# Twenty-five chunks of 504 or 496 tokens in place of 26 of 480, with every product of two layers issued as two of half the columns

## The chip, the core and the metric

The kernel runs on one core of a Trainium2 chip. The metric is the device time of one execution in microseconds (us). Before the change it is 1017.22 us, the median of three runs (1015.54 to 1017.41).

## The reference, cut to what matters

12480 tokens of 128 channels pass through an attention over 32 inducing points and then through two layers with a hidden width of 2048:

```
h = mab(inducing, x)                        # softmax over all 12480 tokens
x = mab(x, h)                               # softmax over the 32 points, per token
h1 = x @ moe_w_in;    x = max(0.01*h1, h1) @ moe_w_out
h2 = x @ moe2_w_in;   g = h2 if h2 >= 1, 0 if h2 <= -1, else (h2+1)**2/4
y  = g @ moe2_w_out
```

## The kernel before

A head reads all tokens once (nine bands) and forms the 32 rows of `h`. The rest works on chunks of 480 tokens, kept with the channels on the partitions and the tokens as columns. There are 26 chunks, and 16 hidden blocks `j` of 128 in each, so the main loop has 26 x 16 steps `k`, called slots here, and 91 more in which the later stages run out.

One slot issues up to ten large products on TensorE, each of a 128-column weight block (96 rows for the first) with a moving operand of 480 columns:

- stage A (L552): one product, `Gs` with `aT`, which gives a hidden block of the first layer. ScalarE writes its ReLU as `hi` (L555), and VectorE (L562) or, in some slots, GpSimd (L560) writes the rest `lo`.
- stage H (L599): three products (`mm3`, L511 to L513) of the hidden block of four slots earlier. They add into a bank `bX` over the 16 slots of a chunk; a 49th product (L601) ends the chunk.
- stage B (L583): three products that give a hidden block of the second layer, for the chunk that stage A began five chunks (86 slots) earlier. VectorE clamps (L585), ScalarE squares (L566), VectorE adds (L589), ScalarE and GpSimd split the result into `hi` and `lo` (L573, L578).
- stage Y (L611): three products of the block of five slots earlier, added into a bank over 16 slots; then a copy and a store (L614, L615).

`mm3` is three products because each operand is a pair of a high and a low part: high by high, low weight by high, high weight by low. All of them have the type fp32r. The attention of the next chunk is spread over the slots of the current one (`attend`, `scores_g`): small products (L447 or L468, L454, L499), and small operations on VectorE and ScalarE.

The order of instructions on each engine is the order in which the loop writes them. So the main loop has three stretches: one in which only A and H run while weights are still converted (slots 0 to 85), one with all four stages, and one with B and Y alone (the last 91 slots). The helper `warm` (L318) in the head issues products of 256 columns whose result nobody reads; they have the same weights each time.

Of the kernel before, what the change touches and what calls it, by code (L numbers as in the profile page):

```python
# [16 lines left out]
PSUM = bass.MemoryType.PSUM  # L17

N, C, M, FF = 12480, 128, 32, 2048
BT = 120  # L20
NB = N // BT
CB = 4
CW = CB * BT
NCH = NB // CB
SC = 4
NSB = -(-NCH // SC)
NJ = FF // 128
K1 = 3 * M
QW = 512
# [10 lines left out]
LAG = 5  # L40
# [30 lines left out]
def moe_kernel(ctx: ExitStack, tc, x_d, xf_d, xl_d, xt_d, it_d, w1_d, w2_d, w3_d, w4_d, y_d):  # L71


    nc = tc.nc
# [10 lines left out]
    bank = [ps.tile([128, 512], F32, name=f"bank{i}", tag=f"bank{i}") for i in range(8)]  # L85
# [82 lines left out]

    def load_xt(c):
        t = xp.tile([C, CW], F32, name="xt")  # L170
        nc.sync.dma_start(out=t, in_=xt_d[:, c * CW:(c + 1) * CW])
        xts[c] = t


# [264 lines left out]
    def scores_g(c, part):  # L439

        b = bX[c % 2]
        if part == 0:
            t = xts.pop(c)
            if c + 1 < NCH:
                load_xt(c + 1)
            for q in range(CB):
                nc.tensor.matmul(b[q * M:(q + 1) * M, :BT], lhsT=HT[:, 0, :], rhs=t[:, q * BT:(q + 1) * BT],  # L447
                                 start=True, stop=True)
        elif part == 1:
            s = at.tile([128, BT], F32, name="sT")  # L450
            nc.scalar.activation(s, b[:, :BT], AF.Copy)
            st[c] = s
        else:
            nc.tensor.transpose(b[:BT, 128:256], st[c], ident)  # L454

    def attend(c, part):

        b = bX[c % 2]
        if c >= GROUPS:
            if part < 3:  # L460
                return scores_g(c, part)
            part -= 2
        if part == 0:
            t = xts.pop(c)
            if c + 1 < NCH:
                load_xt(c + 1)
            for q in range(CB):
                nc.tensor.matmul(b[:BT, q * M:(q + 1) * M], lhsT=t[:, q * BT:(q + 1) * BT], rhs=HT[:, 0, :],  # L468
                                 start=True, stop=True)
        elif part == 1:  # L470
            at0 = 128 if c >= GROUPS else 0
            sv = b[:BT, at0:at0 + CB * M].rearrange("p (b m) -> p b m", m=M)
            m = at.tile([BT, CB], F32, name="m")
            nc.vector.tensor_reduce(out=m, in_=sv, op=ALU.max, axis=AX.X)
            e = at.tile([BT, CB, M], F32, name="ea")
            nc.vector.tensor_tensor(out=e, in0=sv, in1=m[:, :, None].to_broadcast([BT, CB, M]), op=ALU.subtract)
            st[c] = e
        elif part == 2:
            nc.scalar.activation(st[c], st[c], AF.Exp, scale=SCALE)
        elif part == 3:  # L480
            e = st[c]
            d = at.tile([BT, CB], F32, name="d")
            nc.vector.tensor_reduce(out=d, in_=e, op=ALU.add, axis=AX.X)
            nc.vector.tensor_scalar(out=d, in0=d, scalar1=EPS, scalar2=None, op0=ALU.add)
            nc.vector.reciprocal(out=d, in_=d)
            nc.vector.tensor_tensor(out=e, in0=e, in1=d[:, :, None].to_broadcast([BT, CB, M]), op=ALU.mult)
        elif part == 4:
            e = st[c]
            s = at.tile([BT, CB, 3, M], F32R, name="s")
            nc.scalar.activation(s[:, :, 1, :], e, AF.Copy)  # L490
            if c == 0:
                nc.scalar.activation(s[:, :, 2, :], e, AF.Copy)
            nc.vector.tensor_tensor(out=s[:, :, 0, :], in0=e, in1=s[:, :, 1, :].bitcast(F32), op=ALU.subtract)
            st[c] = s
        elif part == 5:
            s = st.pop(c)
            r = 2 if c else 3
            for q in range(CB):
                nc.tensor.matmul(b[:r * M, q * BT:(q + 1) * BT], lhsT=s[:, q, :r].rearrange("p r m -> p (r m)"),  # L499
                                 rhs=identr[:BT, :BT], start=True, stop=True)  # L500
        elif part == 6:
            t = ap.tile([K1, CW], F32R, name="aT")
            r = 2 if c else 3
            nc.scalar.activation(t[:r * M], b[:r * M, :CW], AF.Copy)
            if c:
                nc.scalar.activation(t[2 * M:], b[M:2 * M, :CW], AF.Copy)
            aT[c] = t

    def mm3(out, n, j, hi, lo, start, stop):
        sl = slice(j * 128, (j + 1) * 128)  # L510
# [22 lines left out]
    for k in range(NS + LAG * NJ + OB + D2):  # L533
# [14 lines left out]
        steps = ATTEND_G if c + 1 >= GROUPS else ATTEND  # L548
        part = steps.index(j) if j in steps and c + 1 < NCH else None
        if in_a:  # L550
            p1 = b1[k % (5 if kb < -2 else 2)][:, :CW]
            nc.tensor.matmul(p1, lhsT=Gs[:, j * 128:(j + 1) * 128], rhs=aT[c], start=True, stop=True)  # L552
            hi = hp1.tile([128, CW], F32R, name="hi1")
            lo = hp1.tile([128, CW], F32R, name="lo1")
            nc.scalar.activation(hi, p1, AF.Relu)  # L555
            h1[k] = hi, lo
            if j in (POOL_LO1 if kb >= 0 else POOL_LO1_FILL if c else POOL_LO1_0):
                r = r1p.tile([128, CW], F32, name="r1")
                nc.scalar.activation(r, p1, AF.Relu)  # L559
                nc.gpsimd.tensor_tensor(out=lo, in0=r, in1=hi.bitcast(F32), op=ALU.subtract)  # L560
            else:
                nc.vector.scalar_tensor_tensor(out=lo, in0=p1, scalar=0.0, in1=hi.bitcast(F32),  # L562
                                               op0=ALU.max, op1=ALU.subtract)
        if kb - 1 in cls:
            sq = ep.tile([128, CW], F32, name="sq")
            nc.scalar.activation(sq, cls.pop(kb - 1), AF.Square, scale=-0.5, bias=half)  # L566
            sqs[kb - 1] = sq
        late = None
        if kb - 2 in gs:
            g = gs.pop(kb - 2)  # L570
            hi = hp3.tile([128, CW], F32R, name="hi3")
            lo = hp3.tile([128, CW], F32R, name="lo3")
            nc.scalar.activation(hi, g, AF.Copy)  # L573
            h3[kb - 2] = hi, lo
            if k >= NS and (kb % DVE_LO3 == 0 or kb > NS - 2):
                late = lo, g, hi
            else:
                nc.gpsimd.tensor_tensor(out=lo, in0=g, in1=hi.bitcast(F32), op=ALU.subtract)  # L578
        if in_b:
            if cb == 0:  # L580
                ensure(2, jb)
            p3 = b3[kb % 3][:, :CW]
            mm3(p3, 1, jb, *x2[cb], True, True)  # L583
            cl = ep.tile([128, CW], F32, name="cl")
            nc.vector.tensor_scalar(out=cl, in0=p3, scalar1=1.0, scalar2=-1.0, op0=ALU.min, op1=ALU.max)  # L585
            cls[kb] = cl
        if kb - 1 in sqs:
            g = ep.tile([128, CW], F32, name="g")
            nc.vector.scalar_tensor_tensor(out=g, in0=b3[(kb - 1) % 3][:, :CW], scalar=-1.0, in1=sqs.pop(kb - 1),  # L589
                                           op0=ALU.max, op1=ALU.add)  # L590
            gs[kb - 1] = g
        if late:
# [2 lines left out]
        if 0 <= kh < NS:  # L595
            if ch == 0:
                ensure(1, jh)
            px = bX[ch % 2][:, :CW]
            mm3(px, 0, jh, *h1.pop(kh), jh == 0, False)  # L599
            if jh == NJ - 1:  # L600
                nc.tensor.matmul(px, lhsT=Qs, rhs=aT.pop(ch), start=False, stop=True)  # L601
                hi = x2p.tile([128, CW], F32R, name="x2hi")
                lo = x2p.tile([128, CW], F32R, name="x2lo")
                nc.scalar.activation(hi, px, AF.Copy)
                nc.vector.tensor_tensor(out=lo, in0=px, in1=hi.bitcast(F32), op=ALU.subtract)
                x2[ch] = hi, lo
        if 0 <= ky < NS:
            if cy == 0:
                ensure(3, jy)
            py = (bank[3 + cy % 2] if cy > NCH - LAG else bY)[:, :CW]  # L610
            mm3(py, 2, jy, *h3.pop(ky), jy == 0, jy == NJ - 1)  # L611
            if jy == NJ - 1:
                y = yp.tile([128, CW], F32, name="y")
                nc.scalar.activation(y, py, AF.Copy)  # L614
                nc.sync.dma_start(out=y_d[:, cy * CW:(cy + 1) * CW], in_=y)  # L615
        if part is not None:
            attend(c + 1, part)
        if k in HIDDEN:
# [59 lines left out]
```

## Time and profile before

| what | value |
|---|---|
| median of three runs | 1017.22 us (1015.54 to 1017.41) |
| profiled execution, first to last instruction | 1015.2 us |
| TensorE with a product under way | 997.9 us, 98% of the span |
| VectorE, ScalarE, GpSimd busy | 835.4, 833.6, 646.4 us |
| granted TensorE clock, mean | 0.997 |

The profiled execution has a span of 1015.2 us; its own whole time is not listed apart, and the three runs lie 0.3 to 2.2 us above that span. Products overlap in the trace: one of 480 columns is recorded as 380 ns long, while the next begins 217 ns after it. So the busy share of TensorE doesn't say how near it is to its limit, and the distance from start to start does.

### The profile page before, as it was taken

What the parts mean: (1) busy time and instruction counts of PE and PEld (TensorE: products, weight loads), DVE (VectorE), ACT (ScalarE), POOL (GpSimd) and SP (SyncE); (2) the same over time, 40 slices, a digit from 0 to 9 for tenths busy, and PEclk for the clock granted to TensorE, in tenths of its full rate; (3) what the DMA queues carried; (4) which work ended last, traced back from release to release, by engine and by line L of the source; (5) the groups of instructions that cost most, each with busy time, mean ns of one, the idle gap of its engine ahead of it and who ended that gap; (6) DMA issues with size and microseconds to landing.
All of it is one profiled execution on the core that took longest, in us unless ns stands there. A gap on an engine that the chain in (4) does not pass through costs nothing.

```text
span 1015.2 us, 15773 instructions
## 1 busy us (share of the span) xinstructions
PE 997.9 (98%) x5032; PEld 837.3 (82%) x5032; DVE 835.4 (82%) x1494; ACT 833.6 (82%) x1615; POOL 646.4 (64%) x533
## 2 busy tenths in 40 slices
PE   8899999999999999999999999999999999999998
PEld 6577777888888888888888888888888888888887
DVE  5769987878878888887887888788788888789997
ACT  5577777888888888888888888888888888889997
POOL 0034556666666666666666666666676667678886
PEclk9999999999999999999999999999999999999999
DMA  9800000000000000000000000000000000000000
GB/s 355 309 13 21 10 21 1 20 1 20 21 1 20 20 20 1 20 21 1 20 21 0 20 20 20 1 20 20 1 20 21 6 6 11 11 11 11 11 10 20
DMA packets 11523, 29.89 MB, mean 29 GB/s; under 512 B 1408, under 2 KB 8064, under 8 KB 10672
## 3 DMA queue, kind: packets, MB, share of 16 engines
q1 hardware_dynamic: 11440, 28.89, 8.0%
q8 instruction: 39, 0.64, 0.3%
q14 instruction: 44, 0.36, 0.1%
HBM read 22.50 MB, written 6.39 MB: 28 GB/s over the span
## 4 chain that ended last, share of the span: by engine, by line
PE 93%; DVE 4%; ACT 2%; POOL 1%; issue 1%; POOLq 0%; ACTq 0%
PE bank L511 26%; PE bank L513 26%; PE bank L512 26%; PE bank L552 9%; DVE lo L562 1%; PE bank L255 1%; PE bank L267 1%; PE bank L300 1%; ACT hi L555 1%; PE bank L447 1%; PE bank L499 1%; PE bank L601 1%; PE bank L468 1%; PE bank L225 0%; PE bank L318 0%
## 5 line engine op out<-in xcount | busy, mean ns | idle before, releaser
L578 POOL TENSOR_TENSOR lo<-g,hi 128x480 fp32r<-128x480 f32 x408 | 499.9, 1228 | 233.0 <-PE bank L512 139.8
L555 ACT ACTIVATE hi<-bank 128x480 fp32r<-128x480 f32 x416 | 235.9, 573 | 121.9 <-PE bank L552 119.5
L513 PE MATMUL bank<-lo,whi 128*128 128x480 f32 x832 | 316.8, 381 | 2.1 <-POOL lo L560 2.1
L511 PE MATMUL bank<-hi,whi 128*128 128x480 f32 x832 | 316.1, 380 | 0.0
L512 PE MATMUL bank<-hi,wlo 128*128 128x480 f32 x832 | 315.9, 380 | 0.0
L566 ACT ACTIVATE sq<-cl,half 128x480 f32<-128x480 f32 x416 | 288.8, 694 | 10.8 <-DVE cl L585 5.7
L585 DVE TENSOR_SCALAR cl<-bank 128x480 f32<-128x480 f32 x416 | 270.1, 649 | 26.5 <-PE bank L513 21.6
L589 DVE SCALAR_TENSOR_TENSOR g<-bank,sq 128x480 f32<-128x480 f32 x416 | 269.8, 649 | 26.5 <-ACT sq L566 25.1
L562 DVE SCALAR_TENSOR_TENSOR lo<-bank,hi 128x480 fp32r<-128x480 f32 x317 | 205.3, 653 | 92.8 <-ACT hi L555 92.7
L573 ACT ACTIVATE hi<-g 128x480 fp32r<-128x480 f32 x416 | 248.5, 597 | 0.7 <-DVE g L589 0.5
L513 PEld LDWEIGHTS bank<-lo,whi 128*128 128x128 f32 x832 | 156.7, 188 | 28.6 <-POOL lo L560 3.7
L512 PEld LDWEIGHTS bank<-hi,wlo 128*128 128x128 f32 x832 | 156.7, 188 | 24.9
L511 PEld LDWEIGHTS bank<-hi,whi 128*128 128x128 f32 x832 | 157.1, 189 | 23.9 <-ACT y L614 0.4
L552 PE MATMUL bank<-aT,Gs 96*128 96x480 f32 x416 | 166.1, 400 | 1.8 <-DVE lo L562 1.1
L560 POOL TENSOR_TENSOR lo<-r,hi 128x480 fp32r<-128x480 f32 x99 | 123.3, 1246 | 62.8 <-ACT r L559 59.5
L511 PE MATMUL bank<-x2hi,whi 128*128 128x480 f32 x416 | 159.1, 383 | 0.6 <-DVE g L589 0.6
L513 PE MATMUL bank<-x2lo,whi 128*128 128x480 f32 x416 | 158.4, 381 | 0.0
L512 PE MATMUL bank<-x2hi,wlo 128*128 128x480 f32 x416 | 157.7, 379 | 0.0
L552 PEld LDWEIGHTS bank<-aT,Gs 96*128 96x128 f32 x416 | 78.5, 189 | 19.5 <-issue 4.3
L511 PEld LDWEIGHTS bank<-x2hi,whi 128*128 128x128 f32 x416 | 79.1, 190 | 12.1 <-DVE g L589 1.8
L512 PEld LDWEIGHTS bank<-x2hi,wlo 128*128 128x128 f32 x416 | 78.9, 190 | 12.1
L513 PEld LDWEIGHTS bank<-x2lo,whi 128*128 128x128 f32 x416 | 78.2, 188 | 12.6
(120 smaller groups left out, 541.6 us busy)
## 6 DMA issues: line engine op xcount, KB each, us to landing
wraw<-in_w SPq DMA_DIRECT2D x16, 512.0 KB, 10.1
xt<-in_xt SPq DMA_DIRECT2D x26, 240.0 KB, 2.6
out_y<-y SPq DMA_DIRECT2D x26, 240.0 KB, 2.0
xb<-in_x SPq DMA_DIRECT2D x5, 1024.0 KB, 14.0
xl<-in_xl SPq DMA_DIRECT2D x1, 1024.0 KB, 15.0
xb<-in_x SPq DMA_DIRECT2D x2, 256.0 KB, 9.1
xb<-in_x SPq DMA_DIRECT2D x1, 512.0 KB, 4.0
xl<-in_xl SPq DMA_DIRECT2D x1, 256.0 KB, 16.0
```

Source lines behind the costliest of these rows:

```text
L511: nc.tensor.matmul(out, lhsT=whi[n][:, sl], rhs=hi, start=start, stop=False)
L512: nc.tensor.matmul(out, lhsT=wlo[n][:, sl], rhs=hi, start=False, stop=False)
L513: nc.tensor.matmul(out, lhsT=whi[n][:, sl], rhs=lo, start=False, stop=stop)
L552: nc.tensor.matmul(p1, lhsT=Gs[:, j * 128:(j + 1) * 128], rhs=aT[c], start=True, stop=True)
L555: nc.scalar.activation(hi, p1, AF.Relu)
L560: nc.gpsimd.tensor_tensor(out=lo, in0=r, in1=hi.bitcast(F32), op=ALU.subtract)
L562: nc.vector.scalar_tensor_tensor(out=lo, in0=p1, scalar=0.0, in1=hi.bitcast(F32), op0=ALU.max, op1=ALU.subtract)
L566: nc.scalar.activation(sq, cls.pop(kb - 1), AF.Square, scale=-0.5, bias=half)
L573: nc.scalar.activation(hi, g, AF.Copy)
L578: nc.gpsimd.tensor_tensor(out=lo, in0=g, in1=hi.bitcast(F32), op=ALU.subtract)
L585: nc.vector.tensor_scalar(out=cl, in0=p3, scalar1=1.0, scalar2=-1.0, op0=ALU.min, op1=ALU.max)
L589: nc.vector.scalar_tensor_tensor(out=g, in0=b3[(kb - 1) % 3][:, :CW], scalar=-1.0, in1=sqs.pop(kb - 1), op0=ALU.max, op1=ALU.add)
```

## The change

The 26 equal chunks become ten of 504 tokens and fifteen of 496, 25 in all. Every tile has the width of the wider chunk, and every instruction is cut to the chunk's own width `w` (`bt`, a quarter of it, in the attention). Each of the large products in the main loop goes through a new function `mm`, which issues it as two, one over each half of the columns, with the same weights. The core of the diff:

```
-BT = 120
-CW = CB * BT
-NCH = NB // CB
+WIDTHS = (504,) * 10 + (496,) * 15
+NCH = len(WIDTHS)
+CW = max(WIDTHS)
+BT = CW // CB
+AT = [sum(WIDTHS[:c]) for c in range(NCH + 1)]
+PARTS = 2
...
+    def mm(out, w, x, start, stop):
+
+        n = x.shape[1]
+        cuts = [n * i // PARTS for i in range(PARTS + 1)]
+        for i, (a, b) in enumerate(zip(cuts, cuts[1:])):
+            nc.tensor.matmul(out[:, a:b], lhsT=w, rhs=x[:, a:b], start=start and i == 0, stop=stop and i == PARTS - 1)
 
     def mm3(out, n, j, hi, lo, start, stop):
         sl = slice(j * 128, (j + 1) * 128)
-        nc.tensor.matmul(out, lhsT=whi[n][:, sl], rhs=hi, start=start, stop=False)
-        nc.tensor.matmul(out, lhsT=wlo[n][:, sl], rhs=hi, start=False, stop=False)
-        nc.tensor.matmul(out, lhsT=whi[n][:, sl], rhs=lo, start=False, stop=stop)
+        mm(out, whi[n][:, sl], hi, start, False)
+        mm(out, wlo[n][:, sl], hi, False, False)
+        mm(out, whi[n][:, sl], lo, False, stop)
...
-            p1 = b1[k % (5 if kb < -2 else 2)][:, :CW]
-            nc.tensor.matmul(p1, lhsT=Gs[:, j * 128:(j + 1) * 128], rhs=aT[c], start=True, stop=True)
-            hi = hp1.tile([128, CW], F32R, name="hi1")
+            w = WIDTHS[c]
+            p1 = b1[k % (5 if kb < -2 else 2)][:, :w]
+            mm(p1, Gs[:, j * 128:(j + 1) * 128], aT[c], True, True)
+            hi = hp1.tile([128, CW], F32R, name="hi1")[:, :w]
...
-                nc.tensor.matmul(px, lhsT=Qs, rhs=aT.pop(ch), start=False, stop=True)
+                mm(px, Qs, aT.pop(ch), False, True)
```

All other lines of the diff put a chunk's own width in the place of the common one: in the loads of `xt`, the attention, the banks' slices, the tiles of the stages and the store of `y`.

## Rows read from the trace of the kernel before

**Rows 1.** The page: busy time by engine, and the span in 40 slices.

```profile
PE 997.9 (98%) x5032; PEld 837.3 (82%) x5032; DVE 835.4 (82%) x1494; ACT 833.6 (82%) x1615; POOL 646.4 (64%) x533
...
PEclk9999999999999999999999999999999999999999
```

**Rows 2.** The page: shares of the chain that ended last.

```profile
PE 93%; DVE 4%; ACT 2%; POOL 1%; issue 1%; POOLq 0%; ACTq 0%
```

**Rows 3.** Busy us (and instructions) of each engine in three stretches, then granted clock.

```profile
75.00:140.00 65.00, 61.62 (x298) 50.03 (x297) 60.08 (x110) 50.49 (x107) 32.66 (x24) 1.00 0.06 16
250.00:850.00 600.00, 600.00 (x2895) 509.09 (x2894) 492.02 (x867) 505.56 (x982) 404.43 (x333) 1.00 0.05 14
895.00:1010.00 115.00, 115.00 (x530) 98.64 (x529) 107.25 (x179) 103.21 (x178) 97.02 (x80) 1.00 0.03 12
```

**Rows 4.** Waits between 250 and 850 us, longest first: the first, and TensorE's longest two.

```profile
POOL lo L578 <- PE bank L512: 115.2, 132, 1.4
...
PEld bank L447 <- issue: 5.7, 17, 0.3
...
PEld bank L499 <- DVE s L493: 4.4, 16, 0.3
```

**Rows 5.** Lines of the code: duration min/median/max in ns, first and last start in us.

```profile
L552 PE MATMUL bank<-aT,Gs x416: 375/382/787, 51.7 to 890.5; 96*128 96x480 f32 x139
...
L601 PE MATMUL bank<-aT,Qs x5: 380/383/385, 77.9 to 146.2; 96*128 96x480 f32 x5
...
L454 PE MATMUL bank<-ident,sT x17: 270/272/273, 262.2 to 839.7; 128*120 128x128 f32 x17
...
L585 DVE TENSOR_SCALAR cl<-bank x416: 637/647/659, 150.7 to 1007.5; 128x480 f32<-128x480 f32 x139
```

**Rows 6.** Timeline of TensorE's products from 889.65 us: first and last of 21.

```profile
889.65 0.38 PE L513 MATMUL bank<-lo,whi 128*128 128x480 f32 x1
...
893.99 0.38 PE L511 MATMUL bank<-hi,whi 128*128 128x480 f32 x1
```

**Rows 7.** Timeline from 400.07 us: products (PE) and weight loads (PEld), two of each.

```profile
400.07 0.38 PE L513 MATMUL bank<-x2lo,whi 128*128 128x480 f32 x1
400.07 0.19 PEld L511 LDWEIGHTS bank<-hi,whi 128*128 128x128 f32 x1
400.29 0.38 PE L511 MATMUL bank<-hi,whi 128*128 128x480 f32 x1
400.29 0.19 PEld L512 LDWEIGHTS bank<-hi,wlo 128*128 128x128 f32 x1
```

**Rows 8.** The 256-column products of `warm`: whole run, then three stretches of the timeline.

```profile
L318 PEld LDWEIGHTS bank<-twice,identr x43: 186/189/336, 8.7 to 48.6; 128*128 128x128 f32 x43
L318 PE MATMUL bank<-twice,identr x43: 274/282/682, 8.7 to 48.7; 128*128 128x256 f32 x43
...
13.29 0.88 PE L318 MATMUL bank<-twice,identr 128*128 128x256 f32 x6
...
45.45 1.11 PE L318 MATMUL bank<-twice,identr 128*128 128x256 f32 x8
...
38.25 0.51 PE L318 MATMUL bank<-twice,identr 128*128 128x256 f32 x3
```

**Rows 9.** Transposes of 128 columns with 128-column weights: timeline, then durations of these.

```profile
22.14 1.91 PE L255 MATMUL bank<-ident,xb 128*128 128x128 f32 x16
...
L255 PE MATMUL bank<-ident,xb x16: 273/273/273, 22.1 to 23.8; 128*128 128x128 f32 x16
```

**Rows 10.** Timeline: 128-column products with narrow weights, first and last of eight.

```profile
70.49 0.22 PE L428 MATMUL bank<-whi,GT 128*64 128x128 f32 x1
...
70.91 0.23 PE L430 MATMUL bank<-wlo,GT 128*32 128x128 f32 x1
```

**Rows 11.** Groups by shape, whole run: 480 and 512 columns on VectorE, ScalarE and GpSimd.

```profile
L585 DVE TENSOR_SCALAR cl<-bank 128x480 f32<-128x480 f32 x416 | 270.1, 649 | 26.5 <-PE bank L513 21.6
...
L119 DVE TENSOR_TENSOR w<-cva,cvb 128x512 f32<-128x512 f32 x4 | 2.7, 683 | 0.0
...
L555 ACT ACTIVATE hi<-bank 128x480 fp32r<-128x480 f32 x416 | 235.9, 573 | 121.9 <-PE bank L552 119.5
...
L260 ACT ACTIVATE xT<-bank 128x512 f32<-128x512 f32 x13 | 7.3, 595 | 3.5 <-PE bank L255 3.4
...
L578 POOL TENSOR_TENSOR lo<-g,hi 128x480 fp32r<-128x480 f32 x408 | 499.9, 1228 | 233.0 <-PE bank L512 139.8 <-ACT hi L573 90.3
...
L124 POOL TENSOR_TENSOR wlo<-cva,cvb 128x512 fp32r<-128x512 f32 x10 | 13.1, 1313 | 10.9 <-PE bank L513 8.6 <-DVE cvb L116 2.0
```

More of the change, by code (lines that the diff above doesn't have):

```diff
@@ L19 @@
 N, C, M, FF = 12480, 128, 32, 2048
-BT = 120
-NB = N // BT
 CB = 4
-CW = CB * BT
-NCH = NB // CB
-SC = 4
-NSB = -(-NCH // SC)
+WIDTHS = (504,) * 10 + (496,) * 15
[4 more added lines that the diff above has]
+PARTS = 2
 NJ = FF // 128
@@ L170, in load_xt @@
         t = xp.tile([C, CW], F32, name="xt")
-        nc.sync.dma_start(out=t, in_=xt_d[:, c * CW:(c + 1) * CW])
+        nc.sync.dma_start(out=t[:, :WIDTHS[c]], in_=xt_d[:, AT[c]:AT[c + 1]])
         xts[c] = t
@@ L441, in scores_g @@
         b = bX[c % 2]
+        bt = WIDTHS[c] // CB
         if part == 0:
@@ L446, in scores_g @@
             for q in range(CB):
-                nc.tensor.matmul(b[q * M:(q + 1) * M, :BT], lhsT=HT[:, 0, :], rhs=t[:, q * BT:(q + 1) * BT],
+                nc.tensor.matmul(b[q * M:(q + 1) * M, :bt], lhsT=HT[:, 0, :], rhs=t[:, q * bt:(q + 1) * bt],
                                  start=True, stop=True)
@@ L450, in scores_g @@
             s = at.tile([128, BT], F32, name="sT")
-            nc.scalar.activation(s, b[:, :BT], AF.Copy)
-            st[c] = s
+            nc.scalar.activation(s[:, :bt], b[:, :bt], AF.Copy)
+            st[c] = s[:, :bt]
         else:
-            nc.tensor.transpose(b[:BT, 128:256], st[c], ident)
+            nc.tensor.transpose(b[:bt, 128:256], st[c], ident)
     def attend(c, part):
         b = bX[c % 2]
+        bt = WIDTHS[c] // CB
         if c >= GROUPS:
@@ L467, in attend @@
             for q in range(CB):
-                nc.tensor.matmul(b[:BT, q * M:(q + 1) * M], lhsT=t[:, q * BT:(q + 1) * BT], rhs=HT[:, 0, :],
+                nc.tensor.matmul(b[:bt, q * M:(q + 1) * M], lhsT=t[:, q * bt:(q + 1) * bt], rhs=HT[:, 0, :],
                                  start=True, stop=True)
@@ L471, in attend @@
             at0 = 128 if c >= GROUPS else 0
-            sv = b[:BT, at0:at0 + CB * M].rearrange("p (b m) -> p b m", m=M)
-            m = at.tile([BT, CB], F32, name="m")
+            sv = b[:bt, at0:at0 + CB * M].rearrange("p (b m) -> p b m", m=M)
+            m = at.tile([BT, CB], F32, name="m")[:bt]
             nc.vector.tensor_reduce(out=m, in_=sv, op=ALU.max, axis=AX.X)
-            e = at.tile([BT, CB, M], F32, name="ea")
-            nc.vector.tensor_tensor(out=e, in0=sv, in1=m[:, :, None].to_broadcast([BT, CB, M]), op=ALU.subtract)
+            e = at.tile([BT, CB, M], F32, name="ea")[:bt]
+            nc.vector.tensor_tensor(out=e, in0=sv, in1=m[:, :, None].to_broadcast([bt, CB, M]), op=ALU.subtract)
             st[c] = e
@@ L481, in attend @@
             e = st[c]
-            d = at.tile([BT, CB], F32, name="d")
+            d = at.tile([BT, CB], F32, name="d")[:bt]
             nc.vector.tensor_reduce(out=d, in_=e, op=ALU.add, axis=AX.X)
@@ L485, in attend @@
             nc.vector.reciprocal(out=d, in_=d)
-            nc.vector.tensor_tensor(out=e, in0=e, in1=d[:, :, None].to_broadcast([BT, CB, M]), op=ALU.mult)
+            nc.vector.tensor_tensor(out=e, in0=e, in1=d[:, :, None].to_broadcast([bt, CB, M]), op=ALU.mult)
         elif part == 4:
             e = st[c]
-            s = at.tile([BT, CB, 3, M], F32R, name="s")
+            s = at.tile([BT, CB, 3, M], F32R, name="s")[:bt]
             nc.scalar.activation(s[:, :, 1, :], e, AF.Copy)
@@ L498, in attend @@
             for q in range(CB):
-                nc.tensor.matmul(b[:r * M, q * BT:(q + 1) * BT], lhsT=s[:, q, :r].rearrange("p r m -> p (r m)"),
-                                 rhs=identr[:BT, :BT], start=True, stop=True)
+                nc.tensor.matmul(b[:r * M, q * bt:(q + 1) * bt], lhsT=s[:, q, :r].rearrange("p r m -> p (r m)"),
+                                 rhs=identr[:bt, :bt], start=True, stop=True)
         elif part == 6:
-            t = ap.tile([K1, CW], F32R, name="aT")
+            t = ap.tile([K1, CW], F32R, name="aT")[:, :CB * bt]
             r = 2 if c else 3
-            nc.scalar.activation(t[:r * M], b[:r * M, :CW], AF.Copy)
+            nc.scalar.activation(t[:r * M], b[:r * M, :CB * bt], AF.Copy)
             if c:
-                nc.scalar.activation(t[2 * M:], b[M:2 * M, :CW], AF.Copy)
+                nc.scalar.activation(t[2 * M:], b[M:2 * M, :CB * bt], AF.Copy)
             aT[c] = t
+    def mm(out, w, x, start, stop):
[3 more added lines that the diff above has]
+            nc.tensor.matmul(out[:, a:b], lhsT=w, rhs=x[:, a:b], start=start and i == 0, stop=stop and i == PARTS - 1)
     def mm3(out, n, j, hi, lo, start, stop):
         sl = slice(j * 128, (j + 1) * 128)
-        nc.tensor.matmul(out, lhsT=whi[n][:, sl], rhs=hi, start=start, stop=False)
-        nc.tensor.matmul(out, lhsT=wlo[n][:, sl], rhs=hi, start=False, stop=False)
-        nc.tensor.matmul(out, lhsT=whi[n][:, sl], rhs=lo, start=False, stop=stop)
+        mm(out, whi[n][:, sl], hi, start, False)
+        mm(out, wlo[n][:, sl], hi, False, False)
+        mm(out, whi[n][:, sl], lo, False, stop)
     attend(0, 0)
@@ L550, in moe_kernel @@
         if in_a:
-            p1 = b1[k % (5 if kb < -2 else 2)][:, :CW]
-            nc.tensor.matmul(p1, lhsT=Gs[:, j * 128:(j + 1) * 128], rhs=aT[c], start=True, stop=True)
-            hi = hp1.tile([128, CW], F32R, name="hi1")
-            lo = hp1.tile([128, CW], F32R, name="lo1")
+            w = WIDTHS[c]
+            p1 = b1[k % (5 if kb < -2 else 2)][:, :w]
+            mm(p1, Gs[:, j * 128:(j + 1) * 128], aT[c], True, True)
+            hi = hp1.tile([128, CW], F32R, name="hi1")[:, :w]
+            lo = hp1.tile([128, CW], F32R, name="lo1")[:, :w]
             nc.scalar.activation(hi, p1, AF.Relu)
@@ L557, in moe_kernel @@
             if j in (POOL_LO1 if kb >= 0 else POOL_LO1_FILL if c else POOL_LO1_0):
-                r = r1p.tile([128, CW], F32, name="r1")
+                r = r1p.tile([128, CW], F32, name="r1")[:, :w]
                 nc.scalar.activation(r, p1, AF.Relu)
@@ L564, in moe_kernel @@
         if kb - 1 in cls:
-            sq = ep.tile([128, CW], F32, name="sq")
-            nc.scalar.activation(sq, cls.pop(kb - 1), AF.Square, scale=-0.5, bias=half)
+            cl = cls.pop(kb - 1)
+            sq = ep.tile([128, CW], F32, name="sq")[:, :cl.shape[1]]
+            nc.scalar.activation(sq, cl, AF.Square, scale=-0.5, bias=half)
             sqs[kb - 1] = sq
@@ L570, in moe_kernel @@
             g = gs.pop(kb - 2)
-            hi = hp3.tile([128, CW], F32R, name="hi3")
-            lo = hp3.tile([128, CW], F32R, name="lo3")
+            hi = hp3.tile([128, CW], F32R, name="hi3")[:, :g.shape[1]]
+            lo = hp3.tile([128, CW], F32R, name="lo3")[:, :g.shape[1]]
             nc.scalar.activation(hi, g, AF.Copy)
@@ L581, in moe_kernel @@
                 ensure(2, jb)
-            p3 = b3[kb % 3][:, :CW]
+            w = WIDTHS[cb]
+            p3 = b3[kb % 3][:, :w]
             mm3(p3, 1, jb, *x2[cb], True, True)
-            cl = ep.tile([128, CW], F32, name="cl")
+            cl = ep.tile([128, CW], F32, name="cl")[:, :w]
             nc.vector.tensor_scalar(out=cl, in0=p3, scalar1=1.0, scalar2=-1.0, op0=ALU.min, op1=ALU.max)
@@ L587, in moe_kernel @@
         if kb - 1 in sqs:
-            g = ep.tile([128, CW], F32, name="g")
-            nc.vector.scalar_tensor_tensor(out=g, in0=b3[(kb - 1) % 3][:, :CW], scalar=-1.0, in1=sqs.pop(kb - 1),
+            sq = sqs.pop(kb - 1)
+            w = sq.shape[1]
+            g = ep.tile([128, CW], F32, name="g")[:, :w]
+            nc.vector.scalar_tensor_tensor(out=g, in0=b3[(kb - 1) % 3][:, :w], scalar=-1.0, in1=sq,
                                            op0=ALU.max, op1=ALU.add)
@@ L597, in moe_kernel @@
                 ensure(1, jh)
-            px = bX[ch % 2][:, :CW]
+            w = WIDTHS[ch]
+            px = bX[ch % 2][:, :w]
             mm3(px, 0, jh, *h1.pop(kh), jh == 0, False)
             if jh == NJ - 1:
-                nc.tensor.matmul(px, lhsT=Qs, rhs=aT.pop(ch), start=False, stop=True)
-                hi = x2p.tile([128, CW], F32R, name="x2hi")
-                lo = x2p.tile([128, CW], F32R, name="x2lo")
+                mm(px, Qs, aT.pop(ch), False, True)
+                hi = x2p.tile([128, CW], F32R, name="x2hi")[:, :w]
+                lo = x2p.tile([128, CW], F32R, name="x2lo")[:, :w]
                 nc.scalar.activation(hi, px, AF.Copy)
@@ L609, in moe_kernel @@
                 ensure(3, jy)
-            py = (bank[3 + cy % 2] if cy > NCH - LAG else bY)[:, :CW]
+            w = WIDTHS[cy]
+            py = (bank[3 + cy % 2] if cy > NCH - LAG else bY)[:, :w]
             mm3(py, 2, jy, *h3.pop(ky), jy == 0, jy == NJ - 1)
             if jy == NJ - 1:
-                y = yp.tile([128, CW], F32, name="y")
+                y = yp.tile([128, CW], F32, name="y")[:, :w]
                 nc.scalar.activation(y, py, AF.Copy)
-                nc.sync.dma_start(out=y_d[:, cy * CW:(cy + 1) * CW], in_=y)
+                nc.sync.dma_start(out=y_d[:, AT[cy]:AT[cy + 1]], in_=y)
         if part is not None:
```

## The prediction

> **What bounds the kernel now.** I read the page first. TensorE has a product under way for 98% of the span, at a granted clock that stays at its upper level (2.4 GHz) in all 40 slices [rows 1], and 93% of the chain that ended last lies on it [rows 2]. Since recorded products overlap, neither number says whether TensorE is the limit or only never quite empty. Three other views settle it by stretch.
>
> The windows come next [rows 3]. Between 250 and 850 us TensorE is covered for all 600 us, while VectorE works 82% of the time, ScalarE 84% and GpSimd 67%. The waits of the same stretch [rows 4] are those of GpSimd, ScalarE and VectorE for TensorE; TensorE's own longest ones come to 5.7 and 4.4 us in 600. So here TensorE alone sets the pace. Between 75 and 140 us VectorE is the fullest, 60.1 of 65 us, with the conversion of the weights beside its share of stage A. Between 895 and 1010 us TensorE is covered throughout and VectorE is at 93%.
>
> The lines give the stretches their lengths [rows 5]. Stage A starts at 51.7 us and issues its last product at 890.5; stage B's first clamp is at 150.7 us. The product that ends a chunk (L601) recurs from 77.9 to 146.2 us, four chunks in 68.3 us, or 1067 ns a slot. The transposed scores (L454) recur from 262.2 to 839.7 us, 16 chunks, which is 36.09 us a chunk or 2256 ns a slot.
>
> The timeline gives the price of a product. Twenty distances from start to start take 893.99 - 889.65 = 4.34 us [rows 6], so 217 ns for 480 columns: 200 ns at one column per cycle of 2.4 GHz, and 17 more. A slot with all stages has 10 products and a sixteenth of an 11th, 10.06 x 217 = 2184 ns. The other 72 ns of the 2256 are the attention's small products. The budget closes, so in this stretch any change in the price of a product reaches the end in full.
>
> The weight load of the next product starts with the product before it (both at 400.07 us) and is recorded as 190 ns long [rows 7]; it lies wholly under a product of 217 ns. This cover is what the change spends.
>
> **What the change removes.** One chunk of 26 goes, with its 16 slots: 161 products. But the columns stay: 12480 in all. Were a product's price strictly proportional to its columns (217/480 = 0.452 ns), nothing would be gained but one chunk's attention, 16 x 72 ns = 1.2 us, and parts of a product that don't scale.
>
> **What it adds.** Each of the 25 x 161 = 4025 products is two, so some 3,900 more products and as many more weight loads. That the second half takes its weights anew, although they are the same, is shown by `warm`: 43 loads stand beside 43 products of one unchanging block [rows 8]. A half has 252 or 248 columns. `warm` is the nearest row, at 256 columns with the same type and a 128-column load before each. Three uninterrupted stretches give, with the last product's 282 ns taken off: (880 - 282)/5 = 120 ns, (1110 - 282)/7 = 118 ns, (510 - 282)/2 = 114 ns. Over their 14 distances the mean is 118.1 ns, or 0.4615 ns a column. I take that: 116.3 ns for 252 columns and 114.4 for 248, so 232.6 and 228.8 ns for a split product. It is 2% above the row of 480 per column.
>
> Both bounds come from rows. Below, no half can be faster than its weight load: 16 transposes with 128-column weights, whose own columns are only 128, follow one another every (1910 - 273)/15 = 109 ns [rows 9]. Above stands the longer of the steady `warm` stretches, 119.6 ns, if that is the load's round trip (a load waits until the product before it has begun) and so doesn't shrink with the columns. TensorE's rate of issue excludes neither: products of 128 columns with weights of 64 and 32 follow every (70.91 - 70.49)/7 = 60 ns, load included [rows 10].
>
> The Trainium skill, page "TensorE: Matmul & The Clock Gate", sections "LDWEIGHTS (loading the stationary operand)" and "Back-to-back issue gap", speaks against the change: a load costs its columns over 1.2 GHz, 107 ns here, however short the product is, and each warm product costs N/2.4 + 2.5 ns. By it a half of 252 columns takes 107.5 ns, barely longer than its load; 4025 added halves of 2.5 ns would be an estimated 10 us. The load agrees with the 109 ns of [rows 9]; the product doesn't, 202.5 ns by the page against 217 [rows 6].
>
> **Other engines.** From 480 to 512 columns VectorE's operations go from 649 to 683 ns, ScalarE's from 573 to 595, GpSimd's from 1228 to 1313 [rows 11]; for 504 columns I take three quarters of each step: 26, 17 and 64 ns. Where TensorE sets the pace they stay under it, for their busy shares of 67 to 84% leave over 350 ns a slot. In the last stretch VectorE's two operations per slot come to some 1340 ns against TensorE's 6 x 228.8 = 1373. The semaphores stay: a consumer waits for the second half alone. The attention's parts, their queues and the loads of `xt` keep their slots, one in 16.
>
> **The sum by stretches.**
>
> - Head: the same work. 0.
> - Slots 0 to 85, where VectorE is fullest: stage A's VectorE share of 13 slots in 16 gets 26 ns dearer, 86 x 0.8 x 26 ns = +1.8 us, with the attention's part +2. TensorE's own dearer products hide here: 4 x 233 + 72 = 1004 ns fit under 1067. Without this cover they would cost up to 86 x 4 x 16 ns = 5 us.
> - Slots with all stages: 330 x 2256 = 744.3 us before, 314 slots after. Of these 74 have 504 columns throughout (10.06 x 232.6 + 72 = 2413 ns), 86 have 496 in A and H (4.06 x 228.8 + 6 x 232.6 + 72 = 2397), 154 have 496 throughout (2374): 178.5 + 206.2 + 365.6 = 750.3 us. +6.0.
> - Run-out: 86 slots of B, 91 of Y and 4 of H, 3 products each, 543 x (228.8 - 217) ns = +6.4 us.
>
> Together +14.4 us. On the profiled span that is 1029.6 us, and the runs lie 0.3 to 2.2 us above it; on the median, 1017.2 + 14.4 = 1031.6. I say 1031. One nanosecond more or less per 252-column half moves the time by about 7 us, and 114.3 ns is the price at which nothing changes.
>
> **The rivals.**
>
> - *The load's round trip becomes the bound.* Every half costs 119.6 ns whatever its columns, a product 239.2. A full slot takes 2479 ns, 314 of them 778.4 us (+34); the run-out +12, the start +2: +48, so 1065 us. For it: the two longer `warm` stretches lie at 118 and 120 and the shortest at 114, so a long train of pairs may settle at the top. Against: the load itself repeats in 109 ns [rows 9], so a 120 ns round trip needs 11 ns of handover that those rows don't show.
> - *Columns alone set the price.* Halves cost 0.452 ns a column, as a product of 480 does: 113.9 and 112.1 ns, still above the load. Full slots then take 735 us (-9), the run-out +4, the start +2: -3 us, 1014 us. For it: 128 columns at 60 ns [rows 10] are 0.47 a column, so hardly any part is fixed, and the shortest `warm` stretch lies there.
> - *The other side: short products run faster per column.* If the 17 ns over 200 arise only in products longer than a half, a half is held by its load alone, 109 to 112 ns. At 112, for both widths, a product is 224 ns: full slots 730.4 us (-14), run-out +4, start +2: -8, 1009 us. At 109, a product is 218 ns: -32, +1, +2, 988 us. It decides below 113.8 ns. Against: of the three `warm` stretches none is as fast, though 256 columns need only 107 ns at one per cycle. The skill's rule of N/2.4 + 2.5 ns (same page) would put a half at 107.5 and so at the load's pace; no row here shows so fast a half.
>
> **How the numbers follow.** I give my forecast (halves of 115 to 118.5 ns, +5 to +30 us) 0.48, the round trip 0.20, columns alone 0.15 and the fast halves 0.17. 0.2% is 2 us, about what a measurement of this kernel can tell from no change. Columns alone straddles it: a third each for faster, same and slower. So faster 0.22, same 0.08, slower 0.70. The range runs from 1006 us, the upper half of the fast case, to 1065, the round trip's price; below and above I leave some 0.1 each. Given that the time gets longer, 1022 to 1065 would hold nearly all.
>
> **What would show it.** Some 8,000 more loads and products than the 5032 of each less what a chunk held; halves that start 116 ns apart, in full slots and in the run-out alike, with the next load starting with each; full slots of about 2400 ns; the slots of the first stretch still near 1090; TensorE without waits, and the others waiting longer for it than in [rows 4]. A distance of 119 to 120 ns for halves of both widths is the round trip, one of 114 and 112 is columns alone, and one of 109 to 112 the fast half. I am wrong in another way if TensorE waits for its instructions between the halves, or if the first stretch, now nearly full on TensorE as well, grows by more than 5 us.

## The result, and the profile after

The changed kernel takes 1028.13 us in the median (1026.26 to 1029.71, four runs) against 1017.32 (1015.54 to 1018.28, four runs). The ratio is 1.0108, with a 95% interval of 1.009 to 1.0126: slower by 10.8 us. The prediction was 1031 us, 14 us slower. The profiled execution is the fastest of the four, with a span of 1024.5 us, 9.3 us over that of before.

The page, by engine, answers to [rows 1]:

```profile
PE 1010.0 (99%) x8883; PEld 986.7 (96%) x8883; DVE 832.8 (81%) x1442; ACT 828.6 (81%) x1556; POOL 646.1 (63%) x513
```

Products and weight loads have gone from 5032 to 8883 each. VectorE's and ScalarE's sums hardly move, while the weight loads are now under way for 96% of the span, up from 82%.

The windows answer to [rows 3] (the last one 10 us later, with the run-out):

```profile
75.00:140.00 65.00, 63.50 (x535) 61.87 (x534) 61.21 (x109) 52.16 (x106) 33.46 (x24) 1.00 0.06 17
250.00:850.00 600.00, 600.00 (x5269) 594.85 (x5269) 482.87 (x820) 492.92 (x928) 397.66 (x315) 1.00 0.05 14
905.00:1020.00 115.00, 115.00 (x1001) 114.75 (x1000) 106.71 (x173) 102.17 (x170) 95.88 (x76) 1.00 0.03 12
```

Between 250 and 850 us TensorE is still covered throughout, and the others have become a little emptier: 482.9 us of VectorE after 492.0, 492.9 of ScalarE after 505.6. The longest wait there, answering to [rows 4], is no longer GpSimd's for TensorE but GpSimd's for ScalarE's `hi`; ScalarE's for TensorE comes next, and TensorE's own are shorter still:

```profile
POOL lo L589 <- ACT hi L584: 161.4, 177, 1.6
ACT hi L565 <- PE bank L516: 97.6, 162, 1.1
...
PEld bank L516 <- issue: 3.1, 16, 0.2
```

The lines that bound the stretches and count the chunks, answering to [rows 5]. All split products now stand under one line, L516, and are told apart by their tiles. L455 is the old L454, here in two windows, first among chunks of 504 and then among those of 496:

```profile
L516 PE MATMUL bank<-aT,Gs x800: 272/279/680, 49.8 to 893.1; 96*128 96x248 f32 x96, 96*128 96x252 f32 x64
...
L597 DVE TENSOR_SCALAR cl<-bank x400: 656/673/684, 151.2 to 1016.5; 128x496 f32<-128x496 f32 x80, 128x504 f32<-128x504 f32 x54
...
L455 PE MATMUL bank<-ident,sT x5: 272/272/273, 190.2 to 343.9; 128*126 128x128 f32 x3, 128*124 128x128 f32 x2
...
L455 PE MATMUL bank<-ident,sT x8: 270/272/273, 573.7 to 839.5; 128*124 128x128 f32 x8
```

A full slot takes (343.9 - 190.2)/64 = 2402 ns at 504 columns (in the last seven of these 64, stage A already has 496) and (839.5 - 573.7)/112 = 2373 at 496, against 2256 before.

The timeline of TensorE's products answers to [rows 6]. Each row joins the two halves of a product; shown are the first and last of 21 in a full slot, then of 21 in the run-out:

```profile
240.96 0.40 PE L516 MATMUL bank<-x2hi,whi 128*128 128x252 f32 x2
...
245.63 0.28 PE L516 MATMUL bank<-x2hi,whi 128*128 128x252 f32 x1
...
949.84 0.40 PE L516 MATMUL bank<-x2lo,whi 128*128 128x248 f32 x2
...
954.45 0.39 PE L516 MATMUL bank<-hi,wlo 128*128 128x248 f32 x2
```

Twenty products take 4.67 us, 233.5 ns each, so 116.8 ns a half of 252 columns; and 4.61 us, 230.5 ns each, so 115.2 ns a half of 248.

### The profile page after: what moved, and what is told of

Its sections match the earlier page's. It is cut to its first block, busy times and chain, and to the rows that moved or that the text cites. A ratio compares the mean times of both kernels' runs of the same rounds, so it can differ in the third digit from the quotient of the medians.

```text
span 1024.5 us, 23284 instructions
## 1 busy us (share of the span) xinstructions
PE 1010.0 (99%) x8883; PEld 986.7 (96%) x8883; DVE 832.8 (81%) x1442; ACT 828.6 (81%) x1556; POOL 646.1 (63%) x513
## 4 chain that ended last, share of the span: by engine, by line
PE 91%; DVE 6%; POOL 1%; ACT 1%; issue 0%; POOLq 0%; ACTq 0%
PE bank L516 86%; DVE lo L572 2%; DVE cvb L111 1%; PE bank L255 1%; PE bank L267 1%; PE bank L300 1%; DVE cva L109 1%; PE bank L448 1%; POOL lo L570 0%; PE bank L501 0%; DVE cvb L116 0%; PE bank L470 0%; PE bank L318 0%; POOL wlo L124 0%; PE bank L289 0%; PE bank L225 0%
## 5 line engine op out<-in xcount | busy, mean ns | idle before, releaser
L589 POOL TENSOR_TENSOR lo<-g,hi 128x496 fp32r<-128x496 f32 (+1 forms) x392 | 499.3, 1276 | 240.3 <-ACT hi L584 203.0
L565 ACT ACTIVATE hi<-bank 128x496 fp32r<-128x496 f32 (+1 forms) x400 | 233.8, 589 | 138.8 <-PE bank L516 134.0
L516 PE MATMUL bank<-lo,whi 128*128 128x248 f32 (+1 forms) x1600 | 315.4, 278 | 1.8 <-POOL lo L570 1.8
L516 PE MATMUL bank<-hi,whi 128*128 128x248 f32 (+1 forms) x1600 | 315.0, 278 | 0.0
L516 PE MATMUL bank<-hi,wlo 128*128 128x248 f32 (+1 forms) x1600 | 314.9, 278 | 0.0
L577 ACT ACTIVATE sq<-cl,half 128x496 f32<-128x496 f32 (+1 forms) x400 | 283.9, 710 | 14.1 <-DVE cl L597 11.6
L597 DVE TENSOR_SCALAR cl<-bank 128x496 f32<-128x496 f32 (+1 forms) x400 | 268.3, 671 | 32.9 <-PE bank L516 24.8
L603 DVE SCALAR_TENSOR_TENSOR g<-bank,sq 128x496 f32<-128x496 f32 (+1 forms) x400 | 267.7, 669 | 26.0 <-ACT sq L577 24.0
L572 DVE SCALAR_TENSOR_TENSOR lo<-bank,hi 128x496 fp32r<-128x496 f32 (+1 forms) x305 | 203.8, 673 | 100.2 <-ACT hi L565 100.0
L516 PEld LDWEIGHTS bank<-lo,whi 128*128 128x128 f32 x1600 | 243.3, 188 | 2.8 <-POOL lo L570 2.6
L584 ACT ACTIVATE hi<-g 128x496 fp32r<-128x496 f32 (+1 forms) x400 | 245.3, 613 | 0.5 <-DVE g L603 0.5
L516 PEld LDWEIGHTS bank<-hi,whi 128*128 128x128 f32 x1600 | 243.0, 188 | 0.2 <-ACT y L630 0.2
L516 PEld LDWEIGHTS bank<-hi,wlo 128*128 128x128 f32 x1600 | 243.1, 188 | 0.0
L516 PE MATMUL bank<-aT,Gs 96*128 96x248 f32 (+1 forms) x800 | 164.8, 288 | 0.8 <-ACT aT L506 0.8
L516 PE MATMUL bank<-x2hi,whi 128*128 128x248 f32 (+1 forms) x800 | 157.9, 279 | 0.7 <-DVE g L603 0.7
L516 PE MATMUL bank<-x2lo,whi 128*128 128x248 f32 (+1 forms) x800 | 157.4, 278 | 0.0
L516 PE MATMUL bank<-x2hi,wlo 128*128 128x248 f32 (+1 forms) x800 | 157.3, 278 | 0.0
L516 PEld LDWEIGHTS bank<-aT,Gs 96*128 96x128 f32 x800 | 122.2, 189 | 6.1 <-issue 4.7
L516 PEld LDWEIGHTS bank<-x2hi,whi 128*128 128x128 f32 x800 | 122.2, 189 | 0.9 <-DVE g L603 0.9
L516 PEld LDWEIGHTS bank<-x2lo,whi 128*128 128x128 f32 x800 | 121.6, 188 | 0.0
L516 PEld LDWEIGHTS bank<-x2hi,wlo 128*128 128x128 f32 x800 | 121.4, 188 | 0.0
## 6 DMA issues: line engine op xcount, KB each, us to landing
xl<-in_xl SPq DMA_DIRECT2D x1, 1024.0 KB, 15.4
```

Of the source, the lines that this page charges most:

```text
L516: nc.tensor.matmul(out[:, a:b], lhsT=w, rhs=x[:, a:b], start=start and i == 0, stop=stop and i == PARTS - 1)
L577: nc.scalar.activation(sq, cl, AF.Square, scale=-0.5, bias=half)
```

## The experiments

**u25: the wider chunks without the split.**

```
-PARTS = 2
+PARTS = 1
```

> 25 chunks of 504 and 496 columns, but each product whole again. Theory (the split is the cost; a product is a fixed part of about 6 ns plus 0.439 ns a column, the line through 480 columns at 217 ns and 252 at 117): 227.5 and 224 ns a product, full slots near 2360 and 2325 ns, 1013 to 1016 us, 2 to 3 us under the kernel before. Rival (the wider, fewer chunks themselves cost): stays at 1022 us or more.

1012.28 us (1009.74 to 1013.31, six runs), ratio 0.9951 to the kernel before (0.9936 to 0.9965): 5 us faster than before. The timeline has 17 distances among products of 504 columns from 241.97 to 245.86 us, 229 ns each, and the transposed scores among the chunks of 496 recur in (828.8 - 568.2)/112 = 2327 ns a slot:

```profile
241.97 0.39 PE L516 MATMUL bank<-x2hi,whi 128*128 128x504 f32 x1
...
245.86 0.39 PE L516 MATMUL bank<-hi,wlo 128*128 128x504 f32 x1
...
L455 PE MATMUL bank<-ident,sT x8: 270/270/273, 568.2 to 828.8; 128*124 128x128 f32 x8
```

So the change is two that pull apart: the chunks give 5 us, and the split costs 15.9 us (1028.13 - 1012.28). The rival that wide chunks cost falls. The gain is 2 us larger than expected; the section on the prediction shows where such an amount lies. This kernel beats both others.

**s26: the split without the wider chunks.**

```
-WIDTHS = (504,) * 10 + (496,) * 15
+WIDTHS = (480,) * 26
```

> 26 chunks of 480 columns as before, with each product split into halves of 240. Theory (fixed part plus columns, the load still hidden): 111.7 ns a half, 223 a product, full slots near 2320 ns, about 1042 us. Rival (a round trip of the load of 117 to 120 ns sets a half's price): 234 to 240 ns a product, full slots of 2430 to 2490 ns, 1080 us or more. Rival (the wider chunks are what costs): no change from before, 1017 us.

1042.11 us (1040.01 to 1042.73, four runs), ratio 1.0242 (1.0227 to 1.0258), where 1042 was expected. Full slots take (822.4 - 562.5)/112 = 2321 ns, and 20 products take 4.51 us, 225.5 ns each:

```profile
240.23 0.39 PE L516 MATMUL bank<-x2hi,whi 128*128 128x240 f32 x2
...
244.74 0.39 PE L516 MATMUL bank<-x2hi,whi 128*128 128x240 f32 x2
```

A round trip of 117 to 120 ns is excluded: a half of 240 columns takes 112.7. Alone the split costs 24.6 us, 8.5 ns a product, against 4.5 ns at 504 columns. So the two parts of the change are not independent. Halves of 240 columns lie nearer to the pace of the weight loads, which t25 and the trains below put at 111 to 112 ns.

**t25: three parts.**

```
-PARTS = 2
+PARTS = 3
-        cuts = [n * i // PARTS for i in range(PARTS + 1)]
+        cuts = [n * i // PARTS // 2 * 2 for i in range(PARTS + 1)]
```

> 25 chunks with each product in three parts of 168, or 164 and 166, columns. If the load's pace is a floor of 109 to 112 ns: 330 ns a product, full slots near 3390 ns, 1400 to 1430 us. If no floor exists and only a fixed part per instruction is paid: 240 ns a product, about 1065 us. With a round trip of 117 to 120 ns: 355 ns a product, full slots near 3650 ns, 1500 us or more.

One run: 1438.73 us, just above the 1400 to 1430 expected of a floor at the load's pace. Each row joins three parts; 17 products take 5.70 us, 335 ns each, so 112 ns a part of 168 columns, which would take 76 ns at the 229/504 ns a column of u25:

```profile
239.83 0.50 PE L516 MATMUL bank<-hi,whi 128*128 128x168 f32 x3
...
245.53 0.50 PE L516 MATMUL bank<-x2hi,whi 128*128 128x168 f32 x3
```

**bench: trains of like products ahead of the head.** A tile `four` holds the identity four times over; the rest is the changed kernel.

```
+    for m in (128, 64):
+        for n in (512, 504, 480, 384, 320, 256, 252, 248, 240, 224, 192, 160, 128, 96):
+            for i in range(24):
+                nc.tensor.matmul(bank[1][:m, :n], lhsT=identr[:, :m], rhs=four[:, :n], start=True, stop=True)
```

> The changed kernel with trains of 24 like products ahead of the head, whose result nobody reads: 14 widths from 512 to 96 columns, with weights of 128 and then of 64 columns. Theory: with 128-column weights the distance falls by 0.44 ns a column from 231 ns at 512 to about 112 at 240 and stays at 109 to 112 below; with 64-column weights it goes on to about 60 ns at 128 columns. Rival (round trip): with 128-column weights 252 columns and fewer stay at 117 to 120. Rival (the load under way slows the columns): 64-column weights give less at 480 columns, 208 ns or below.

One run, 1122.33 us, the trains included. Timeline rows of seven trains, first with weights of 128 columns, then of 64:

```profile
11.95 5.60 PE L232 MATMUL bank<-four,identr 128*128 128x504 f32 x24
...
33.10 2.96 PE L232 MATMUL bank<-four,identr 128*128 128x252 f32 x24
...
38.62 2.87 PE L232 MATMUL bank<-four,identr 128*128 128x240 f32 x24
...
49.33 2.83 PE L232 MATMUL bank<-four,identr 128*128 128x128 f32 x24
...
60.21 5.62 PE L232 MATMUL bank<-four,identr 128*64 128x504 f32 x24
...
81.39 2.89 PE L232 MATMUL bank<-four,identr 128*64 128x252 f32 x24
...
95.92 1.60 PE L232 MATMUL bank<-four,identr 128*64 128x128 f32 x24
```

A row's time, less one product's own (the mean of its train: 388, 279, 276 and 274 ns in the first group, 390, 276 and 223 in the second), over its 23 distances gives 227, 117, 113 and 111 ns with 128-column weights, and 227, 114 and 60 with 64. So 128-column loads have a floor of 111 ns, half as many columns a lower one; at 504 columns the load's width makes no difference here, and at 252 it makes 3 ns of 117. So in the trains the load under way doesn't slow the columns of a long product.

**narrow2 and narrow1: loads of 64 columns in the kernel itself.** From the trains I took the load's pace, close under the halves, to be the split's whole cost. In both kernels stages H, B and Y take 64 weight columns and leave out half of their outputs, while stage A keeps 128; narrow1 also has `PARTS = 1`.

```
-    def mm(out, w, x, start, stop):
+    def mm(out, w, x, start, stop, m=64):
...
-            nc.tensor.matmul(out[:, a:b], lhsT=w, rhs=x[:, a:b], start=start and i == 0, stop=stop and i == PARTS - 1)
+            nc.tensor.matmul(out[:m, a:b], lhsT=w[:, :m], rhs=x[:, a:b], start=start and i == 0, stop=stop and i == PARTS - 1)
...
-            mm(p1, Gs[:, j * 128:(j + 1) * 128], aT[c], True, True)
+            mm(p1, Gs[:, j * 128:(j + 1) * 128], aT[c], True, True, 128)
```

> The changed kernel, halves and all, but stages H, B and Y load 64 of the 128 weight columns and write 64 partitions of their banks; half of the outputs of those stages are left out, and stage A stays whole. In the trains such a load repeats in 58 ns in place of 112, and 252 columns cost 113.5 ns in place of 116.5. Theory now (a half costs 0.45 ns a column like a whole product, and what it costs beyond that is the 112 ns pace of the 128-column load close under it): halves of 113.5 and 112 ns, full slots near 2350 ns with 504 columns, 1010 to 1016 us. Rival (a fixed part of 5 to 6 ns in every product instruction): halves stay at 117 and 115 ns, full slots at 2405, 1026 to 1030 us.

> The same 64 weight columns with each product whole, as a control: half of the outputs of stages H, B and Y are left out. Both theories: a load under a product of 229 ns has room whatever its width, so 229 and 225 ns a product, full slots near 2360 and 2327 ns, 1010 to 1014 us as with 128 columns. If the load under way slows the columns themselves: 224 ns or less a product, 995 us or less.

narrow2 takes 1021.81 us (1020.13 to 1023.2, seven runs), ratio 1.0052 (1.0038 to 1.0065); narrow1 takes 1008.4 (1006.9 to 1008.84, four runs), ratio 0.9914 (0.9895 to 0.9933). The slots among the chunks of 496, narrow2 first:

```profile
L455 PE MATMUL bank<-ident,sT x8: 270/270/273, 573.8 to 837.6; 128*124 128x128 f32 x8
```

```profile
L455 PE MATMUL bank<-ident,sT x8: 270/270/272, 566.5 to 826.3; 128*124 128x128 f32 x8
```

They are 2355 and 2320 ns, so with narrow loads the split costs 35 ns a slot, or 3.5 ns in each of 10.06 products, where it cost 2373 - 2327 = 46 ns, or 4.6, with loads of 128 columns. In time it is 13.4 us instead of 15.9, with the heads in it, which differ; from stage A's first product on, the traces have (1020.9 - 53.1) - (1006.9 - 50.8) = 11.7 us instead of (1024.5 - 49.8) - (1010.1 - 50.8) = 15.4. My theory from the trains falls, for narrow2 was to take 1010 to 1016 us; but the rival's 1026 to 1030 is missed as well. The load's pace is about a quarter of what the split costs at these widths. The rest is still there with narrow loads. Whether it belongs to the added product or to the added load, which always come together, no run tells.

narrow1 came out below its 1010 to 1014 us too: its whole products cost 7 ns a slot less than those of u25, 0.7 ns each. So in the kernel a load of 128 columns, or the outputs that go with it, costs a long product 0.3%, far less than the 5 ns or more of the rival.

**w512: wider halves.**

```
-WIDTHS = (504,) * 10 + (496,) * 15
+WIDTHS = (512,) * 16 + (480,) * 8 + (448,)
```

> The changed kernel with 16 chunks of 512, eight of 480 and one of 448 columns, so halves of 256, 240 and 224. Theory now: the wider a half, the less of the load's pace shows: 256 columns cost 117 to 118 ns, 1.5 to 2.5 over half a whole product of 231; 240 cost 113 as in the kernel of 26 split chunks; 224 cost 112 to 113. Full slots of 2440 and 2330 ns, 1028 to 1036 us. Rival (fixed part): 118.7, 111.7 and 104.6 ns.

One run: 1036.01 us. Of 22 distances among products of 512 columns the timeline shows:

```profile
239.84 0.39 PE L516 MATMUL bank<-hi,whi 128*128 128x256 f32 x2
...
245.08 0.41 PE L516 MATMUL bank<-lo,whi 128*128 128x256 f32 x2
```

5.24 us, 238.2 ns a product, 119.1 ns a half. That speaks against the theory once more, which had 117 to 118; the fixed part's line gave 118.7. The last chunk, with halves of 224 columns, speaks the other way:

```profile
1023.81 0.39 PE L516 MATMUL bank<-x2hi,whi 128*128 128x224 f32 x2
...
1029.40 0.39 PE L516 MATMUL bank<-hi,wlo 128*128 128x224 f32 x2
```

25 distances take 5.59 us, 223.6 ns a product, 111.8 ns a half: the floor of the theory (112 to 113), and not the 104.6 of a fixed part alone. So both are there: the fixed part in wider halves, the floor from some 240 columns down.

## Why the prediction came out

**TensorE's products are the bound, and each step in their price reaches the end.** Right. In every kernel the time follows the product's price: 225.5 ns at 480 columns split gives 1042 us, 233.5 and 230.5 give 1028, 229 whole gives 1012.

**The price of a half.** It was taken as 116.3 and 114.4 ns from the 256-column products of `warm`; it measures 116.8 and 115.2. Full slots came to 2402 and 2373 ns where 2413 and 2374 were written. That they came so near is partly luck, twice over. Products of 256 columns take 119.1 ns in the kernel (w512), not the 118.1 of the three `warm` stretches, and scaled from that the half of 252 would have been 117.2. And the halves were taken too cheap, but the attention's rest too dear: 10.06 products of 233.5 or 230.5 ns leave 53 or 54 ns of a slot, where 72 were kept.

**What a half pays beyond its columns.** The prediction took the price from a row and named no mechanism for it. The line through 504 columns at 229 ns (u25) and 252 at 116.8 has 0.445 ns a column and 4.6 ns fixed; it is a fit within about 1 ns, with 218 at 480, where [rows 6] have 217, and 115 at 248. Below it lies the floor of 111 to 112 ns, which a half of 240 columns (112.7) nearly touches and halves of 224 and thirds of 168 don't pass. narrow2 shows that the nearness of this floor accounts for about a quarter of the split's cost at 248 columns; the rest, 3.5 ns a product, is what I call the fixed part. What it consists of isn't settled: in the trains with 64-column weights it is nearly absent (2 x 114 ns against 227), in the kernel it is there.

**The rivals.** The round trip at 119.6 ns for all widths is excluded by s26, whose halves take 112.7. Columns alone is excluded by the 4.5 ns between a split and a whole product of 504. Halves held by the load alone, at 109 to 112 ns, are excluded by the run itself. Two sums of this last rival are off in the prediction, without changing a verdict: at 109 ns the full slots come to -33 us, not -32, and by the same terms a price common to both widths shortens the time below 113.1 ns, not 113.8. The page "TensorE: Matmul & The Clock Gate" of the Trainium skill, section "LDWEIGHTS (loading the stationary operand)", puts a load at its columns over 1.2 GHz, 107 ns for 128; the trains and t25 agree nearly, at 111 and 112. The N/2.4 + 2.5 ns of the same page of the Trainium skill, section "Back-to-back issue gap", gives 212.5 at 504 columns against the 229 measured.

**The sum by stretches**, from the starts in [rows 5] and in the same lines after, where 14.4 us were predicted and 9.3 came in the profiles:

| stretch | before, us | after, us | difference | predicted |
|---|---|---|---|---|
| head, to stage A's first product | 51.7 | 49.8 | -1.9 | 0 |
| to stage B's first clamp | 99.0 | 101.4 | +2.4 | +2 |
| to stage A's last product | 739.8 | 741.9 | +2.1 | +6.0 |
| run-out | 124.7 | 131.4 | +6.7 | +6.4 |

The first stretch and the run-out came as priced; in the first, TensorE's dearer products hid as expected: u25, with whole products, takes no less there, 103.0 us (153.8 - 50.8), though its trace begins that stretch at the lower clock, 0.61 from 50 to 54 us. Two terms were mis-sized. The head was given no difference and became 1.9 us shorter, and the step for the full slots was 3.9 us too large. In both places TensorE had run at its lower clock before, and didn't after.

The windows of before, first in the head and then where stage B begins:

```profile
8.00:14.00 6.00, 5.67 (x46) 4.18 (x47) 2.97 (x9) 2.23 (x7) 0.00 (x0) 0.72 0.99 412
...
157.00:164.00 7.00, 5.40 (x16) 4.33 (x17) 5.31 (x11) 4.80 (x10) 3.74 (x4) 0.76 0.01 2
```

and the same windows of after:

```profile
8.00:14.00 6.00, 6.00 (x55) 4.66 (x55) 3.65 (x11) 3.14 (x9) 0.00 (x0) 1.00 1.00 418
...
157.00:164.00 7.00, 6.32 (x55) 6.12 (x55) 6.83 (x13) 5.70 (x11) 5.55 (x5) 1.00 0.01 2
```

The third column from the end is the granted clock: 0.72 and 0.76 before, 1.00 after. With two levels, 2.4 and 1.2 GHz, about half of either stretch ran at the lower one. I had read [rows 3] from windows that leave both places out, and the page's slices of 25 us [rows 1] hide them.

What it cost in the head shows in the time between the same two products, before and then after:

```profile
8.34 0.42 PE L267 MATMUL bank<-xT,iT 128*32 128x128 f32 x8 [0.78 <-DVE xT L258]
...
14.13 1.91 PE L255 MATMUL bank<-ident,xb 128*128 128x128 f32 x16
```

```profile
7.56 0.43 PE L267 MATMUL bank<-xT,iT 128*32 128x128 f32 x8 [0.78 <-DVE xT L258]
...
12.20 1.91 PE L255 MATMUL bank<-ident,xb 128*128 128x128 f32 x16
```

It is 5.79 us before and 4.64 after, so 1.15 of the 1.9 us. The other 0.8 lies ahead of it, in 20 transposes from 1.36 us on that took 4.51 us before and 3.73 after. Nothing in the head was changed, and its length differs from one trace to the next: stage A starts at 49.8 us in the changed kernel, at 50.6 in s26 and at 53.1 in narrow2. Without the head the profiles lie 11.2 us apart, as the medians do (10.8).

At 157 us there is more to it. Before, TensorE had waited twice there:

```profile
157.96 0.48 PE L552 MATMUL bank<-aT,Gs 96*128 96x480 f32 x1 [1.10 <-DVE lo L562]
159.08 0.59 PE L511 MATMUL bank<-x2hi,whi 128*128 128x480 f32 x1 [0.65 <-DVE g L589]
...
162.67 0.44 PE L552 MATMUL bank<-aT,Gs 96*128 96x480 f32 x1
```

After, it waited once:

```profile
158.89 0.50 PE L516 MATMUL bank<-x2hi,whi 128*128 128x252 f32 x2 [0.68 <-DVE g L603]
```

Before, the nine products from 159.08 to 162.67 us follow one another every 399 ns instead of 217, which makes 1.6 us at the lower clock. With the wait of 1.10 us that is 2.7 of the 3.9 us. The 74 slots of 2402 ns in place of 2413 make an estimated 0.8 more; 0.4 us stay open.

s26 has the same two waits (0.90 and 0.64 us) and the same granted clock of 0.76 in this window; the changed kernel, u25, narrow1, narrow2 and w512, all of 25 chunks, have only the second wait, of 0.68 us, and a clock of 1.00. So the longer wait and the lower clock go with the 26 chunks of 480 in these seven traces. That the wait brings the lower clock is not shown, and the chunks alone don't: two of the four runs of s26 have a granted clock of 1.0 over the whole run. What made the longer wait, the last section tells. The 2 us by which u25 beat its expectation are of this size; that they lie here is not shown.

## What to carry to other kernels

Where TensorE is the bound, price a product by its distance from start to start and not by its recorded length; here it was 4.6 ns and 0.445 ns a column, so fewer and wider products gain and splitting them loses. A product shorter than its weight load (112 ns for 128 columns of fp32r) is paid at the load's price, and one a few per cent longer already pays some of it. When a change does two things, run each alone: here one of them gave 5 us (of which some 2.7 may be the wait and the clock at 157 us), and the kernel with that one alone beats both others.

## What the runs showed of the hardware that was not expected

A small VectorE operation took over four times as long where a GpSimd operation had begun just before it. In the kernel before, the elementwise product L486 of 120x128, whose lateness made the longer wait above, took 1.35 us from 155.98 us; GpSimd's operation had started at 155.97. After, its counterpart L488 started first, by 0.03 us, and took 0.29:

```profile
L486 DVE TENSOR_TENSOR ea<-ea,d x26: 291/293/1349, 49.3 to 847.8; 120x128 f32<-120x128 f32 x26
...
155.97 1.22 POOL L578 TENSOR_TENSOR lo<-g,hi 128x480 fp32r<-128x480 f32 x1 [0.26 <-ACT hi L573]
155.98 1.35 DVE L486 TENSOR_TENSOR ea<-ea,d 120x128 f32<-120x128 f32 x1
```

```profile
156.77 0.29 DVE L488 TENSOR_TENSOR ea<-ea,d 126x128 f32<-126x128 f32 x1
156.80 1.40 POOL L589 TENSOR_TENSOR lo<-g,hi 128x504 fp32r<-128x504 f32 x1 [0.30 <-ACT hi L584]
```

Of the 26 operations of L486 five take 1.31 to 1.35 us, and each of the five starts 15 to 52 ns after a GpSimd operation has begun; the other 21 start with none under way and take 0.29. The GpSimd operation that came second, after, took 1.40 us, where the mean of its kind is 1.29. So the order of two starts, some 10 to 30 ns apart, decided a microsecond. In s26 GpSimd was first again (156.34 us, VectorE 156.35), and the product took 1.35. The Trainium skill, page "SBUF — State Buffer", section "SBUF: two separate sides", says that a VectorE operation with two inputs in SBUF and a GpSimd operation that reads SBUF lock each other out of a shared port pair for a whole instruction; the times here agree, 1.35 us being the 1.22 of the one and part of the other, but no run was made to try it.

And halves of 256 columns, at 119.1 ns, lie 0.6 ns above the 118.5 of the line through 252 and 504 columns; why is open.
